# A residual layer scale on one core: the second of two early loads issued behind the entry barriers

## The chip, the cores and the metric

The kernel runs on one core of one Trainium2 chip. The metric is the device time of one execution in microseconds; the time before is 119.91 us, the median of 3 runs (119.89 to 119.97). The profile is of one more execution, whose span from the first to the last instruction of the program is 118.6 us, at a granted clock of 1.0.

## The reference

```python
B, S, D = 1024, 16, 512
x, y:  (B, S, D) bfloat16
gamma: (D,)      bfloat16

def reference(x, y, gamma):
    return x + gamma * y
```

Flattened, x, y and the output are 16,384 rows of 512 numbers, 16.78 MB each. Two are read and one is written: 50.33 MB in all. The arithmetic is one multiplication and one addition per element.

## The kernel before

Each of the 128 partitions gets 128 rows, in blocks of 8, 60 and 60. The transfers are two lists, one for SP's queue and one for the queue of ScalarE; an entry is a kind, and the rows from and to. VectorE has a list too: a multiplication ("m") in place in y_sb and an addition ("a") of x, piece by piece.

```python
BLOCKS = [8, 60, 60]
PIECES = [8, 15, 45, 60]

SP = [
    ('y', 0, 8),          # 1 MB, the first load
    ('y', 8, 68),         # 7.86 MB, the second load
    ('x', 8, 68, 0),
    ('y', 68, 128),
    ('x', 68, 128, 15),
    ('x', 0, 8, 0),
]
ACT = [('g',), ('s', 8, 68), ('s', 68, 128), ('s', 0, 8)]
EARLY = (2, 0)            # how many of SP's and of ScalarE's list go ahead of all else
HOLD = ('y', 0, 8)        # what lets the others go
RELEASE = ('x', 68, 128, 15)
DVE = [('m', 0), ('m', 1), ('m', 2), ('a', 2), ('a', 1), ('m', 3), ('a', 3), ('a', 0)]
```

The helper `ring` writes out one list. The entries from number n_early on are held behind a semaphore; the stores wait for `s_go` and for the additions.

```python
def ring(eng, what, n_early):
    known, went = 0, False
    for k, w in enumerate(what):
        kind = w[0]
        if k == n_early:
            _take(s_held[eng], 1, eng)       # wait for it, then take it back
        ...                                  # waits for buffers, additions, s_go
        elif kind == "y":
            r = slice(w[1], w[2])
            i = eng.dma_start(out=y_sb[:, r, :], in_=rows_of(yf, w[1], w[2])).then_inc(s_load[w], 16)
        ...
        if k < n_early:
            early.append(i.ins)

ring(nc.sync, SP, EARLY[0])
ring(nc.scalar, ACT, EARLY[1])
```

TensorE lets the held ones go when the first load has landed. It also spreads gamma over the partitions, by a product of a row of ones with gamma's row:

```python
nc.vector.memset(ones_row, 1.0).then_inc(s_ones, 1)
_take(s_load[HOLD], 16, nc.tensor)           # the first load has landed
for s_one in s_held.values():
    nc.tensor.sem_inc(s_one, 1)              # SP, ScalarE, VectorE may go on
_take(s_ones, 1, nc.tensor)
_take(s_gamma, 16, nc.tensor)
nc.tensor.matmul(gamma_ps, ones_row, gamma_row, start=True, stop=True).then_inc(s_ps, 1)
```

The program begins with entry barriers, at which all five engines wait for one another several times. They are not written in the kernel; they stand in the program's first block, with four small memsets on GpSimd. The last lines of the kernel take the early transfers out of its own block, which lies behind the barriers, and put them at the head of the first block, ahead of the barriers:

```python
main = nc.main_func.blocks[0].instructions
names = {i.name for i in early}
for b in nc.main_func.blocks[1:]:
    for i in [i for i in b.instructions if i.name in names]:
        b.instructions.remove(i)
for k, i in enumerate(early):
    main.insert(1 + k, i)
```

Of the kernel before, what the change touches and what calls it, by code (L numbers as in the profile page):

```python
# [11 lines left out]
SP = [  # L12
    ('y', 0, 8),
    ('y', 8, 68),
# [4 lines that stand above are left out]
]  # L19
ACT = [('g',), ('s', 8, 68), ('s', 68, 128), ('s', 0, 8)]  # L20

EARLY = (2, 0)

HOLD = ('y', 0, 8)

RELEASE = ('x', 68, 128, 15)

# [4 lines left out]
def _take(sem, n, eng):  # L32


    return eng.wait_ge(sem, n).then_inc(sem, -n)  # L35


def kernel(
# [9 lines left out]
    nc = tc.nc  # L48
# [16 lines left out]
    def rows_of(t, a, b):  # L65

        c = max(c for c in range(len(BLOCKS)) if edges[c] <= a)
        assert b <= edges[c + 1]
        block = t[P * edges[c] : P * edges[c + 1]].rearrange("(p n) d -> p n d", p=P)
        return block[:, a - edges[c] : b - edges[c], :]  # L70
# [25 lines left out]
    def pieces_of(a, b):  # L96
        return [c for c in range(n) if meets(starts[c], starts[c + 1], a, b)]
# [4 lines left out]
    def frees(w):  # L102

        c = set()
        for v in x_loads[: x_loads.index(w)]:
            lo, hi = max(v[3], w[3]), min(v[3] + v[2] - v[1], w[3] + w[2] - w[1])
            if lo < hi:
                c |= set(pieces_of(v[1] + lo - v[3], v[1] + hi - v[3]))
        return sorted(c)

    early = []

    def ring(eng, what, n_early):

        known, went = 0, False
        for k, w in enumerate(what):
            kind = w[0]
            if k == n_early:
                _take(s_held[eng], 1, eng)
            need = frees(w) if kind == "x" else pieces_of(w[1], w[2]) + list(w[3:]) if kind == "s" else []  # L120
            need = max((order[c] + 1 for c in need), default=0)
            if kind == "s" and not went:
                _take(s_go, 1, eng)
                went = True
            if need > known:
                eng.wait_ge(s_add, need)
                known = need
            if kind == "g":
                i = eng.dma_start(out=gamma_row, in_=gamma.unsqueeze(0)).then_inc(s_gamma, 16)
            elif kind == "x":  # L130
                to = x_sb[:, w[3] : w[3] + w[2] - w[1], :]
                i = eng.dma_start(out=to, in_=rows_of(xf, w[1], w[2])).then_inc(s_load[w], 16)
# [3 lines that stand above are left out]
            else:  # L136
                r = slice(w[1], w[2])
                i = eng.dma_start(out=rows_of(of, w[1], w[2]), in_=y_sb[:, r, :]).then_inc(s_out, 16)
            if k < n_early:
                early.append(i.ins)  # L140

    ring(nc.sync, SP, EARLY[0])
    ring(nc.scalar, ACT, EARLY[1])


    nc.vector.memset(ones_row, 1.0).then_inc(s_ones, 1)  # L146
    _take(s_load[HOLD], 16, nc.tensor)
    for s_one in s_held.values():
# [14 lines left out]
    def need(loads, c):  # L163
        for w in loads:
            if w not in landed and meets(starts[c], starts[c + 1], w[1], w[2]):
                if w == RELEASE:
                    _take(s_rel, 1, nc.vector)
                elif w == HOLD:
                    _take(s_held[nc.vector], 1, nc.vector)
# [64 lines left out]
```

## Time and profile before

| What | Value |
|---|---|
| Time, median of 3 | 119.91 us |
| Span of the profiled execution | 118.6 us |
| VectorE busy | 70.1 us (59%) |
| Moved by DMA | 50.33 MB, mean 424 GB/s over the span |
| First load: issued, landed | 0.00 us, 4.90 us |
| Second load: issued, landed | 0.42 us, 23.03 us |
| Last store: issued, landed | 96.52 us, 118.61 us |

In the profile's lines DVE is VectorE, PE is TensorE, POOL is GpSimd, SP and ACT are SyncE and ScalarE; a "q" behind a name is the engine's sequencer, which waits, passes barriers and issues transfers and is not counted as busy. L135 is a load of y, L132 of x, L129 of gamma, L138 a store, L35 a wait in the helper `_take`. L218 and L51 are the places of the entry barriers, their drains and their events. DMA packets are booked in the window in which they start. A line of the view by source begins with the line, engine and operation, then durations in ns (least, median, most), then the first and last start in us.

### The profile page before, as it was taken

To read this page: it belongs to the slowest core of one execution; us is meant where nothing else is said; L and a number is where in the kernel's file an instruction comes from. 1 tells how busy PE (TensorE), PEld (TensorE's weight loads), DVE (VectorE), ACT (ScalarE), POOL (GpSimd) and SP (SyncE) were. 2 spreads that over 40 slices of the span, in tenths; PEclk is the share of its full clock that TensorE was granted. 3 is DMA by queue.
4 is the path that set the end of the run, shared out by engine and by line. 5 is a ranking of instruction groups with operands and counts; after the bars stand their busy time and mean duration, and the time that the engine had idled before them with its cause. 6 is when DMAs were issued, how large, how long until landed. Compare 5 with 4: busy or idle time off the path is not lost. (4 is left out here: it accounts for less than half of the span.)

```text
span 118.6 us, 87 instructions
## 1 busy us (share of the span) xinstructions
PE 0.6 (0%) x1; PEld 0.1 (0%) x1; DVE 70.1 (59%) x10; POOL 0.2 (0%) x4
## 2 busy tenths in 40 slices
PE   0001000000000000000000000000000000000000
PEld 0000000000000000000000000000000000000000
DVE  0000720199999399999499999569999950000000
POOL 0000000000000000000000000000000000000000
DMA  5999799779779879879977977897997797797787
GB/s 182 503 560 435 331 394 601 331 331 663 331 331 642 352 331 621 373 331 394 601 331 331 663 331 331 384 633 331 414 580 331 331 663 331 331 663 331 331 367 318
DMA packets 1298, 50.33 MB, mean 424 GB/s; under 512 B 145, under 2 KB 146, under 8 KB 146
## 3 DMA queue, kind: packets, MB, share of 16 engines
q1 hardware_dynamic: 864, 33.55, 65.8%
q10 hardware_dynamic: 434, 16.78, 32.7%
HBM read 33.56 MB, written 16.78 MB: 424 GB/s over the span
## 5 line engine op out<-in xcount | busy, mean ns | idle before, releaser
L180 DVE TENSOR_TENSOR y_sb<-y_sb,gamma_sb 128x4096 bf16<-128x4096 bf16 (+3 forms) x4 | 34.7, 8690 | 9.7 <-DVEq L35 9.7
L189 DVE TENSOR_TENSOR y_sb<-x_sb,y_sb 128x23040 bf16<-128x23040 bf16 (+3 forms) x4 | 34.6, 8688 | 4.5 <-DVEq L35 4.5
L154 DVE CAST gamma_sb<-gamma_ps 128x512 bf16<-128x512 f32 x1 | 0.7, 692 | 10.1 <-DVEq L35 10.1
L146 DVE MEMSET ones_row<- 1x128 bf16 x1 | 0.2, 165 | 2.0 <-PEq L51 2.0
L152 PE MATMUL gamma_ps<-gamma_row,ones_row 1*128 1x512 bf16 x1 | 0.6, 578 | 11.6 <-PEq L35 11.6
L152 PEld LDWEIGHTS gamma_ps<-gamma_row,ones_row 1*128 1x128 bf16 x1 | 0.1, 100 | 11.5 <-issue 11.5
L218 POOL MEMSET const-uint8-127<- 128x1 uint8 x1 | 0.1, 102 | 0.0
L218 POOL MEMSET const-bfloat16-1.0<- 128x1 bf16 x1 | 0.1, 101 | 0.0
L218 POOL MEMSET const-float32-0.0<- 128x1 f32 x1 | 0.1, 98 | 0.2 <-issue 0.2
L218 POOL MEMSET const-float32-1.0<- 128x1 f32 x1 | 0.1, 98 | 0.0
## 6 DMA issues: line engine op xcount, KB each, us to landing
y_sb<-in_y_dram SPq DMA_DIRECT2D x2, 7680.0 KB, 38.2
x_sb<-in_x_dram SPq DMA_DIRECT2D x2, 7680.0 KB, 29.9
out_dram<-y_sb ACTq DMA_DIRECT2D x2, 7680.0 KB, 21.0
y_sb<-in_y_dram SPq DMA_DIRECT2D x1, 1024.0 KB, 4.9
x_sb<-in_x_dram SPq DMA_DIRECT2D x1, 1024.0 KB, 22.3
out_dram<-y_sb ACTq DMA_DIRECT2D x1, 1024.0 KB, 22.1
gamma_row<-in_gamma_dram ACTq DMA_DIRECT2D x1, 1.0 KB
```

The source lines that it names most:

```text
L146: nc.vector.memset(ones_row, 1.0).then_inc(s_ones, 1)
L152: nc.tensor.matmul(gamma_ps, ones_row, gamma_row, start=True, stop=True).then_inc(s_ps, 1)
L154: nc.vector.tensor_copy(out=gamma_sb, in_=gamma_ps).then_inc(s_dve, 1)
L180: nc.vector.tensor_tensor(out=yt, in0=yt, in1=g, op=MULT).then_inc(s_dve, 1)
L189: nc.vector.tensor_tensor(out=yt, in0=xt, in1=yt, op=ADD).then_inc(s_add, 1)
L218: nc = _bacc.Bacc("TRN2", target_bir_lowering=False, num_devices=1)
```

## The change

Only one load instead of two is put ahead of the barriers. The hold stays where it was, ahead of the third entry: it gets a number of its own, AHEAD. The second load is thus issued in the kernel's own block, behind the barriers, without waiting for any semaphore of the kernel. Its place in SP's order stays the same. It is meant to let SP come to the barriers sooner, with only the first load's issue ahead of them.

```diff
-EARLY = (2, 0)
-
-HOLD = ('y', 0, 8)
+EARLY = (1, 0)
+
+HOLD, AHEAD = ('y', 0, 8), (2, 0)
 ...
-    def ring(eng, what, n_early):
+    def ring(eng, what, n_early, n_ahead):
 ...
-            if k == n_early:
+            if k == n_ahead:
                 _take(s_held[eng], 1, eng)
 ...
-    ring(nc.sync, SP, EARLY[0])
-    ring(nc.scalar, ACT, EARLY[1])
+    ring(nc.sync, SP, EARLY[0], AHEAD[0])
+    ring(nc.scalar, ACT, EARLY[1], AHEAD[1])
```

SP's instructions then stand in this order: first load, barriers and branch, second load, wait for the hold, x load, and so on. The other engines' instructions are the same as before.

## The prediction, made before the changed kernel was run

> **What bounds the kernel now.** I read the page from the top: busy times first, then the slices, then the queues. They say at once that no engine bounds this kernel. The busiest is VectorE:
>
> ```profile
> PE 0.6 (0%) x1; PEld 0.1 (0%) x1; DVE 70.1 (59%) x10; POOL 0.2 (0%) x4
> ...
> DMA  5999799779779879879977977897997797797787
> ...
> q1 hardware_dynamic: 864, 33.55, 65.8%
> q10 hardware_dynamic: 434, 16.78, 32.7%
> ```
>
> Queue q1 carries the loads (two tensors of 16.78 MB), q10 gamma and the stores. Together they fill 65.8 + 32.7 = 98.5% of the 16 DMA engines' time over the span. The sevens in the row of slices are no idle time: a packet of 61,440 bytes takes 2.27 us and is booked where it starts, so a slice of 3 us catches one or two rounds of them. Over a longer stretch this averages out. The view by windows (columns: stretch, length, busy time of PE, PEld, DVE and POOL, clock, DMA share, GB/s) gives:
>
> ```profile
> 0.00:1.00 1.00, 0.00 (x0) 0.00 (x0) 0.00 (x0) 0.20 (x4) 1.00 0.00 0
> ...
> 1.00:2.00 1.00, 0.00 (x0) 0.00 (x0) 0.01 (x1) 0.00 (x0) 1.00 0.74 131
> ...
> 2.00:118.60 116.60, 0.58 (x1) 0.10 (x1) 70.11 (x10) 0.00 (x0) 1.00 1.00 431
> ```
>
> The reader is to see three things. In the first microsecond no byte moves. In the second, packets are open but only 131 GB/s flow. From 2.0 us on, the DMA share is 1.00 up to the end, at 431 GB/s. So the kernel is 50.33 MB of traffic behind a start-up of about 2 us, and only what delays the start of that stream, or tears a hole in it, can change the time.
>
> The page's chain of the work that ended last covers only 16% of the span (issue 12%, DVE 4%), because it doesn't follow the transfers; I leave it aside. What VectorE waits for shows in the groups, and it has slack: its last addition ends at 96.48 us, and the last 38.6 us (from the landing of the last load at 79.96 us) are stores alone: 16.78 MB / 38.6 us = 435 GB/s, the full rate.
>
> The start is in the timeline (start, duration, engine, operation):
>
> ```profile
> 0.00 0.85 SPq L135 DMA_DIRECT2D y_sb<-in_y_dram  x2
> ...
> 1.99 0.17 DVE L146 MEMSET ones_row<- 1x128 bf16 x1 [1.99 <-PEq L51]
> 5.23 0.33 SPq L132 DMA_DIRECT2D x_sb<-in_x_dram  x1
> 5.43 0.52 ACTq L129 DMA_DIRECT2D gamma_row<-in_gamma_dram  x1
> ```
>
> Both early loads are issued before the barriers (0.00 to 0.37 and 0.42 to 0.85 us). VectorE passes the barriers at 1.9 us and does its memset. Nothing else is issued until the first load, 1 MB, has landed at 4.90 us.
>
> And the entry barrier waits for SP, which comes late because it issues two transfers first:
>
> ```profile
> L218 PEldq DRAIN  x1: 8/8/8, 0.3 to 0.3; - x1
> ...
> L218 SPq DRAIN  x1: 125/125/125, 0.9 to 0.9; - x1
> ```
>
> The other engines are at their drain by 0.3 us (GpSimd's ends at 0.48), SP's runs from 0.90 to 1.03 us. The barriers that follow take from there to 1.84 us on SP.
>
> **What the Trainium skill says.** "DMA: Bandwidth & Descriptors", section "Queues, rings and completion order", says that each issuing engine owns one ring on each of the 16 DMA engines and that descriptors are consumed in ring order. The trace agrees: on all 16 engines the first load's eight packets of 8,192 bytes come first, then those of the second load. The second load therefore can't start earlier than the first is through, however early it was issued. "Perfetto Trace Analysis", section "DMA Instruction — HWDGE (DVE, Sync)", says that the recorded span of an issuing instruction is the making of descriptors, and that data moves after or beside it; here the issue lasts 0.37 us and the first packet starts at 1.02 us. "DMA: Bandwidth & Descriptors", section "Latency and other measured facts", puts the first byte of such a transfer at about 0.6 us; 1.02 - 0.37 = 0.65 us agrees.
>
> **The change, part by part.**
>
> 1. *It removes* one issue of 0.42 us, plus a gap of 0.05 us, from SP's way to the first barrier. SP's drain then starts near 0.43 instead of 0.90 us. GpSimd's drain at 0.48 becomes the last to arrive, or close to it, so the barriers end some 0.45 us earlier: 1.84 - 0.45 = 1.4 us on SP. This is worth nothing by itself. Behind the barriers lie only a memset and waits that the first load ends at 4.9 us.
>
> 2. *It moves* the second issue to behind the last barrier. VectorE shows what a step out of it costs: 0.13 us from its last barrier event to its memset. So the issue runs from about 1.5 to 1.9 us, against 0.42 to 0.85 before, 1.1 us later.
>
> 3. *When do its descriptors stand in the rings?* Take the pattern of the first load, the only one issued to idle DMA engines: eight engines start a packet 1.02 to 1.09 us after the issue began, the other eight 1.71 to 1.82 us after. For the second load that gives 1.5 + 1.0 = 2.5 us to 1.5 + 1.8 = 3.3 us.
>
> 4. *When are they needed?* In the trace's packets, each engine ends its eight packets of the first load between 4.17 and 4.55 us and takes a packet of 61,440 bytes at once. Margin: 4.17 - 3.3 = 0.9 us on the worst pairing of engines, 4.17 - 2.5 = 1.7 us on the better one. Neither is used up, so no hole opens.
>
> 5. *Everything after* hangs on the first load's landing (4.90 us) and on the order in SP's ring, which stays the same: second load, then x, then the third load of y. Nothing moves.
>
> Sum: 0 from the barriers, 0 from the later issue. 119.91 us stays 119.9, with one open term that the next part names.
>
> **The rivals.**
>
> *A: a hole between the first and the second load.* If the second issue comes later than 1.5 us, or its descriptors take longer than the first load's, engines stand idle from 4.2 us until they arrive. Every microsecond of that goes whole into the end. For it: the first load is short, 1 MB, some 2.4 us at full rate. Against it: it takes 0.9 us more delay than I reckon before the first engine runs dry. A miss by 1.2 us would make 120.2 us.
>
> *B: the start of the first load becomes faster.* Half of the engines start their first packet only at 1.71 us or later, and the eight early ones hold theirs for 0.97 to 1.30 us where every later one takes 0.31. In just this time, from 0.42 us, SP has the second transfer's descriptors made. If these two are in each other's way, the change frees the first load, it lands earlier than 4.90 us, and the whole stream moves up with it: 0.1 to 0.6 us, so 119.3 to 119.8 us. For it: the coincidence in time. Against it: all 16 engines are through their first packet between 2.03 and 2.31 us whether they began early or late, which looks like one common latency of a first read, not a queue for descriptors. I think this likelier than A, which puts the middle slightly under the time before.
>
> *C: the earlier barriers bring something.* Then the memset at 1.99 us would have to matter. It doesn't: TensorE needs it only with gamma, which lands at 11.43 us, and VectorE's first multiplication at 13.24 us is 105 us ahead of the end, with transfers saturated throughout. This rival makes no difference to the time.
>
> **Range and chances.** The centre is 119.91 minus 0.06 for B at small odds: 119.85 us. Downward the range holds most of B (half a microsecond: 119.4); upward a small hole or a slightly different rate (0.3 us: 120.2). To leave the 2% band it would take 2.4 us, more than the whole start-up lasts, or a hole as long as the whole first load; 1% on either side is ample.
>
> **What would show it.** In the changed profile: SP's drain near 0.4 us and VectorE's memset near 1.5 us (step 1); one issue at 0.00 and one at about 1.5 us (step 2); window 2.0 us to the end at a DMA share of 1.00 and 431 GB/s (steps 3 and 4); the first load landing at 4.9 us and the x issue at 5.2 us (step 5). A share under 1.00 between 4 and 10 us would prove A; a landing of the first load at 4.3 to 4.8 us, with all engines started by 1.5 us, would prove B. The prediction is wrong if the second issue lands far behind 1.5 us, or if the two issues do disturb each other by more than half a microsecond.

## The result, and the profile after

The changed kernel takes **121.62 us** (median of 6 runs, 121.12 to 121.69) against 119.96 us before in the same runs (119.89 to 120.11). The ratio is 1.0128, with a 95% interval of 1.011 to 1.0147: slower by 1.7 us, outside the predicted range of 119.4 to 120.2 us.

The page of the changed kernel, in the lines that answer to those shown of before:

```profile
PE 0.6 (0%) x1; PEld 0.1 (0%) x1; DVE 70.1 (58%) x10; POOL 0.2 (0%) x4
...
q1 hardware_dynamic: 864, 33.55, 65.2%
q10 hardware_dynamic: 434, 16.78, 32.4%
```

The work is the same to a tenth of a microsecond. The queues fill 97.6% of the span in place of 98.5%: 1.8 us longer, with the same bytes. Its timeline and its view by source of the barrier's lines show that what I predicted of the issues came true:

```profile
0.00 1.76 SPq L135 DMA_DIRECT2D y_sb<-in_y_dram  x2
...
1.52 0.17 DVE L146 MEMSET ones_row<- 1x128 bf16 x1 [1.52 <-PEq L51]
5.24 0.33 SPq L132 DMA_DIRECT2D x_sb<-in_x_dram  x1
```

```profile
L218 SPq DRAIN  x1: 131/131/131, 0.4 to 0.4; - x1
```

SP drains at 0.42 us, VectorE's memset comes at 1.52 us (1.99 before), the second load is issued from 1.43 to 1.76 us, and x at 5.24 us, as before. (The timeline joins both loads into one row of 1.76 us.) What I predicted of the stream did not: from 2.0 us to the end the DMA share is 0.98 at 423 GB/s, and not 1.00 at 431.

```profile
2.00:120.40 118.40, 0.58 (x1) 0.10 (x1) 69.96 (x9) 0.00 (x0) 1.00 0.98 423
```

The sign that I had named for rival A, a share under 1.00 between 4 and 10 us, would have missed it. Before, then after:

```profile
4.00:10.00 6.00, 0.00 (x0) 0.00 (x0) 0.00 (x0) 0.00 (x0) 1.00 1.16 501
```

```profile
4.00:10.00 6.00, 0.00 (x0) 0.00 (x0) 0.00 (x0) 0.00 (x0) 1.00 1.06 431
```

Since a packet is booked whole where it starts, so short a window can read over 1.00 although engines stand idle in it. Only the comparison with before shows that something is missing. Windows chosen to fit the rounds of packets find the time in two places. From 4.60 to 6.20 us nothing may start, because each engine should be inside its first packet of 61,440 bytes; before, then after:

```profile
4.60:6.20 1.60, 0.00 (x0) 0.00 (x0) 0.00 (x0) 0.00 (x0) 1.00 0.00 0
```

```profile
4.60:6.20 1.60, 0.00 (x0) 0.00 (x0) 0.00 (x0) 0.00 (x0) 1.00 0.14 38
```

38 GB/s over 1.6 us is 61 KB: one engine takes up its first packet of the second load only now (at 5.11 us in the packet records). The second place lies 75 us later; again before, then after:

```profile
79.40:80.40 1.00, 0.00 (x0) 0.00 (x0) 1.00 (x1) 0.00 (x0) 1.00 1.00 430
```

```profile
79.40:80.40 1.00, 0.00 (x0) 0.00 (x0) 0.53 (x1) 0.00 (x0) 1.00 0.28 115
```

There most DMA engines stand idle for a microsecond, between the loads and the stores. (0.28 counts the packets that start there; with each packet spread over its duration, the engines are busy for 0.39 of that microsecond.)

I added up the packets of both traces, each spread over its duration, and compared when the same amount had been moved:

| Moved | Before | After | Behind |
|---|---|---|---|
| 1 MB | 4.18 us | 4.08 us | -0.09 us |
| 2 MB | 6.50 us | 6.89 us | 0.39 us |
| 4 MB | 11.11 us | 11.63 us | 0.52 us |
| 32 MB | 75.71 us | 76.18 us | 0.47 us |
| 34 MB | 80.37 us | 81.59 us | 1.22 us |
| 50 MB | 117.25 us | 118.60 us | 1.35 us |
| last store landed | 118.61 us | 120.32 us | 1.71 us |

Half a microsecond is lost where the engines pass from the first to the second load (below: the handover), nothing for 28 MB, 0.75 us where they pass from loads to stores (the seam), 0.13 us in the stores, and 0.36 us at the end, where the last engine lags.

The lag begins at the handover. The 16 engines report the second load's landing one by one: before, 22.65 to 23.03 us, all within 0.38 us; after, 22.73 to 23.50 us for 15 of them, and 24.77 us for the last, 1.27 us behind the fifteenth. This distance stays: 1.27, 1.28 and 1.29 us at the next three loads. Nobody takes over the late engine's work in these loads. The last of these loads is the one that lets the stores go. It landed at 79.23 us on the last engine and at 77.94 us on the fifteenth. The stores were therefore issued at 79.58 us, and their first packet came 0.87 us later, when most engines had run dry.

### The profile page after: what moved, and what is told of

The parts are those of the page before. It is cut to its first block, busy times and chain, and to the rows that moved or that the text cites. A ratio compares the mean times of both kernels' runs of the same rounds, so it can differ in the third digit from the quotient of the medians.

```text
span 120.4 us, 87 instructions
## 1 busy us (share of the span) xinstructions
PE 0.6 (0%) x1; PEld 0.1 (0%) x1; DVE 70.1 (58%) x10; POOL 0.2 (0%) x4
```

## The experiments

In the tables "extra" is by how much the first packet of 61,440 bytes lasted longer than the usual 2.27 us, in the mean of the 16 engines, from the packet records (2.23 us for packets of 60,416 bytes, 2.12 us for 57,344). It is the profiled execution's; times are medians of several. It leaves out time in which an engine stood idle ahead of that packet, so it is a sign of the loss at the handover and not its size: in a second profile of the changed kernel it is only 0.16 us, although the stream was 0.58 us behind at 4 MB. In the diffs, `...` marks lines left out, and the line that allocates `s_pad` is shown once.

### Place or moment?

`both_behind` issues both loads behind the barriers; `apart_ahead` issues both ahead of them, with a pause between.

```diff
 both_behind, against the changed kernel
-EARLY = (1, 0)
+EARLY = (0, 0)
 apart_ahead, against the changed kernel
-EARLY = (1, 0)
+EARLY = (2, 0)
+PADS = 24
 ...
+    s_pad = sem("s_pad")          # a semaphore that nothing waits for
 ...
+            if k == 1 and eng is nc.sync:
+                early.extend(eng.sem_inc(s_pad, 1).ins for _ in range(PADS))
```

> Both early loads are issued behind the entry barriers, 0.4 us apart as in the kernel before; nothing is left ahead of the barriers. Theory 'gap' (the second load's descriptors need some 2.6 to 3.5 us from the issue until data flows, on one engine nearly 5 us, and the first load is through before that when its issue is 1.4 us earlier): here the two issues are close together again, so no engine falls behind; the 16 landings of the second load lie within 0.4 us of one another and the time is that of the kernel before plus the later start, 120.0 + 1.4 = 121.4 us. Theory 'place' (a transfer issued behind the barriers is served worse): an engine falls behind as in the changed kernel and the time is over 122.3 us. Theory 'stream' (making descriptors while the engines move data disturbs them): as 'gap', for no data moves at the second issue.

> Both early loads stand ahead of the barriers as in the kernel before, but 24 increments of an unused semaphore on SP stand between their issues, so that the second one comes about 1 us later (some 1.4 to 2 us after the first). Theories 'gap' and 'stream': an engine falls behind by about a microsecond at the second load, its landings spread over 1 to 2 us, and the time is 121 to 122 us. Theory 'place': 119.9 to 120.1 us, as in the kernel before, with landings within 0.4 us.

`both_behind` took 121.27 us, ratio 1.011 (1.0093 to 1.0127): just the later start. Its timeline:

```profile
1.38 0.85 SPq L135 DMA_DIRECT2D y_sb<-in_y_dram  x2
1.47 0.17 DVE L146 MEMSET ones_row<- 1x128 bf16 x1 [1.47 <-PEq L51]
6.50 0.33 SPq L132 DMA_DIRECT2D x_sb<-in_x_dram  x1
```

Both issues stand together again, 1.38 us later than before, and 119.93 + 1.38 = 121.31. The extra is 0.00 us and the second load's landings lie within 0.55 us (I had expected 0.4), as wide as the first load's own. `apart_ahead` issued the second load at 1.83 us and took 120.84 us (11 runs, 120.08 to 121.54), ratio 1.0075 (1.0049 to 1.01), extra 0.45 us. Its median lies just under what I expected, and its spread is wide. So the barriers are not needed for the loss: it comes with the time between the two issues alone. To be sure, the same moment as in the changed kernel, but ahead of the barriers (17 increments):

> The same with 17 increments: the second load is issued at about 1.43 us, the moment at which the changed kernel issues it, but ahead of the barriers and not behind them. If the moment is all that counts: as the changed kernel, 120.9 to 121.7 us with landings of the second load spread by 0.7 us or more. If standing behind the barriers adds something of its own: under 120.5 us.

121.24 us, ratio 1.0111 (1.007 to 1.0152), issued at 1.43 us, extra 0.51 us. It is a loss like the changed kernel's without the change of place; its four runs lie from 120.63 to 121.90 us. Its window:

```profile
4.60:6.20 1.60, 0.00 (x0) 0.00 (x0) 0.00 (x0) 0.00 (x0) 1.00 0.62 230
```

230 GB/s over 1.6 us is 368 KB: six engines begin late here, and not one.

And with the same distance, both behind the barriers:

```diff
 against apart17
-EARLY = (2, 0)
+EARLY = (0, 0)
 ...
-                early.extend(eng.sem_inc(s_pad, 1).ins for _ in range(PADS))
+                for _ in range(PADS):
+                    eng.sem_inc(s_pad, 1)
```

> Both loads behind the barriers with 17 increments between them, so the second one is issued about 1.4 us after the first, which itself starts at 1.4 us. With both close together behind the barriers the time was 121.27 us. If the limit is the distance from the first issue: the loss comes on top, 0.7 to 1.9 us, 122.0 to 123.1 us. If the limit were tied to the start of the program and not to the first issue: 121.2 to 121.5 us.

122.53 us, ratio 1.0229 (1.0197 to 1.0262), extra 0.68 us: the loss, 1.26 us against `both_behind`, comes on top of the later start. The limit moves with the first issue, or with the first packets, which start 1.0 us after it in both kernels, and not with the start of the program.

### Where is the limit?

The same kernel with 8, 12 and 45 increments in place of 24.

> As the run with both loads ahead of the barriers and 24 increments between them, but with 8 increments: the second load is issued at about 0.9 us, some 3.3 us before the first engine is through with the first load (4.17 us before). Theory 'gap' with a need of 2.6 to 3.5 us on most engines: nearly no loss, 119.9 to 120.4 us. If any distance of more than the 0.4 us of before hurts: 120.6 us or more.

> Both loads ahead of the barriers, 12 increments between them: the second load is issued at about 1.14 us. With 8 increments (0.91 us) nothing was lost, with 24 (1.83 us) 0.9 us. If the limit is the first packets' start at 1.0 us: a loss already, 120.4 to 121.2 us. If the limit is a distance of some 3 us to the end of the first load at 4.17 us: just no loss, 119.9 to 120.2 us.

> As before, with 45 increments: the second load is issued at about 3.05 us, 1.1 us before the first engine is through. Theory 'gap' as a plain latency of some 3.3 us: the stream stands still until about 6.4 us and loses some 2.1 us, so 121.9 to 122.5 us. If the loss at the second load is a fixed cost of a start while other packets flow, and not a latency from the issue: 120.5 to 121.5 us, as with 24 increments.

| Second issue at | Time | Ratio (95%) | Extra |
|---|---|---|---|
| 0.91 us | 119.94 us | 1.0001 (0.9993 to 1.001) | 0.03 us |
| 1.13 us | 120.00 us (20 runs) | 1.0035 (1.0015 to 1.0055) | 0.00 us |
| 1.43 us | 121.24 us | 1.0111 (1.007 to 1.0152) | 0.51 us |
| 1.83 us | 120.84 us | 1.0075 (1.0049 to 1.01) | 0.45 us |
| 3.06 us | 120.77 us | 1.0073 (1.0057 to 1.0089) | 0.50 us |

At 0.91 us the second load's delay costs nothing. At 1.13 us the runs fall into two groups: 12 of 20 at 119.87 to 120.08 us, 8 at 120.70 to 121.31 us (the profiled one is of the first group). From 1.43 us on every run is slower than the slowest of before in the same series, but for one at 1.83 us that equals it. The first load's first packets start at 0.99 to 1.02 us in these traces, so the edge lies close to the moment at which the engines begin to work. Whether that moment makes it, or the distance between the issues, these runs don't separate. Both expectations for 1.13 us were half right, in different runs. For 3.06 us my main expectation was wrong: 1.2 us later than 1.83 us, and no dearer. It isn't a plain latency from the issue, which would have grown with every microsecond.

When the second load's data began to flow shows it better. I estimate that moment for each engine by taking the usual 2.27 us back from the end of its first long packet. Before, it is 4.2 to 4.6 us. With the second issue at 1.43, 1.83 and 3.06 us it is 4.6 to 5.6, 4.2 to 5.4 and 4.5 to 5.2 us: nearly the same moment, within about a microsecond of the first load's last packets (they end at 3.9 to 4.5 us), whatever the issue. In the last of these that is only 1.5 to 2.1 us after the issue.

### Is it a matter of distance to the end of the first load?

The first load gets 16 rows (2 MB) in place of 8; and once 10 rows.

```diff
 big_before and big_after: EARLY = (2, 0) and (1, 0)
-BLOCKS = [8, 60, 60]
-PIECES = [8, 15, 45, 60]
+BLOCKS = [16, 56, 56]
+PIECES = [16, 16, 40, 56]
 big_apart57 and big_apart80: the same with EARLY = (2, 0), PADS = 57 and 80
 first10: EARLY = (1, 0)
+BLOCKS = [10, 59, 59]
+PIECES = [10, 15, 44, 59]
 (the two lists' rows follow)
```

> The first load is 16 rows (2 MB) in place of 8, the other blocks 56 rows each; both early loads ahead of the barriers. It is the other half of the next run. All theories: landings of the second load within 0.5 us; the time near that of the kernel before, 119.7 to 120.5 us.

> As the run before it (first load of 2 MB), with the second load issued behind the barriers. The engines are busy with the first load until about 6.6 us, so the second load's descriptors have 5 us from their issue at 1.4 us. Theory 'gap': they are there in time; within 0.2 us of the run before it, and no engine behind. Theory 'stream' (descriptors are made while the engines move data, whatever the margin): 0.7 to 1.7 us slower than the run before it, with an engine behind. Theory 'place': the same as 'stream'.

> The changed kernel with a first load of 10 rows in place of 8 (the other blocks 59 rows each). The second load is issued at 1.42 us as in the changed kernel, but the engines are busy with the first load until about 4.8 us, so the distance from the issue to the end of the first load is 3.4 us and not 2.8 us. Theory 'distance' (no loss where the second load is issued 3.3 us or more before the first load ends, a loss of 0.5 to 0.9 us below some 2.8 us): no loss at the start, 119.9 to 120.3 us. Rival 'before the first packet' (the second load has to be issued before the first packets flow at 1.0 us, unless the first load is very long): 120.6 us or more, with the window from 4 to 9 us at less than a DMA share of 1.00 or landings of the second load spread by over 0.7 us.

> The 2 MB first load again, both loads ahead of the barriers, with 57 increments between them: the second load is issued at about 3.75 us, some 2.9 us before the engines are through with the first load at 6.6 us. Theory 'distance': the loss comes back, 0.4 to 0.9 us over the same kernel without the increments (120.63 us): 121.0 to 121.6 us. If a long first load hides the second one's start whatever the distance: 120.5 to 120.9 us.

> The 2 MB first load with 80 increments: the second load is issued at about 5.1 us, 1.5 us before the first engines are through with the first load. With 57 increments (2.9 us) the change from the first to the second load cost nothing. A latency of 2 to 3 us from the issue: the loss is there, 0.5 us or more between the second and the fourth megabyte, 121.5 us or more. If long packets at the end of the first load hide the start at any distance: the change still costs nothing, 120.7 to 121.4 us.

| Kernel | Second issue at | First engine takes up the second load at | Time | Ratio (95%) | Extra |
|---|---|---|---|---|---|
| big_before | 0.42 us | 6.40 us | 120.63 us | 1.006 (1.0045 to 1.0075) | 0.00 us |
| big_after | 1.42 us | 6.63 us | 120.81 us | 1.0077 (1.0062 to 1.0092) | 0.00 us |
| big_apart57 | 3.77 us | 6.63 us | 121.18 us | 1.0105 (1.0086 to 1.0124) | 0.00 us |
| big_apart80 | 5.60 us | 6.60 us | 121.89 us | 1.0183 (1.0134 to 1.0233) | 0.29 us |
| first10 | 1.43 us | 4.70 us | 120.39 us | 1.0042 (1.0025 to 1.0058) | 0.16 us |

With the 2 MB load the change as such costs next to nothing: 120.81 against 120.63 us, intervals that overlap, no extra. (This layout is itself 0.7 us slower than the 1 MB one; why stays open.) Here the second issue falls while packets flow, so making descriptors beside moving data doesn't cost anything by itself: the theory 'stream' of the expectations falls. But a rule of distance, counted from the second issue to the moment at which the first engine is free for it, fails too. 2.9 us were enough here (57 increments), while with 10 rows 3.3 us left an extra of 0.16 us, and 2.3 us in the changed kernel (3.70 less 1.43 us) left 0.53. (How much of the 0.4 us by which `first10` is slower is its layout's is not shown: there is no run of it with both loads early.) With 80 increments the second load was issued later than I had reckoned, 1.0 us ahead of that moment, and the extra is back; its data began to flow 1.5 to 2.1 us after the issue, as with the issue at 3.06 us above. In its profile about 0.3 us are lost at the handover and 1.2 us at the seam, where `big_before` loses 0.5. So a longer first load hides the start of the second; how much time it needs isn't one number. `big_apart57` lost 0.55 us against `big_before` all the same: in its profile one engine starts the first load itself only at 2.24 us and lands 0.7 us behind the others. That lag doesn't come from the handover and stays unexplained.

### Other causes that were tried

Three other transfers are issued at 5.2 to 6.1 us, just when the second load begins. `quiet` puts them off:

```diff
+    for _ in range(20):
+        nc.tensor.sem_inc(s_pad, 1)
     for s_one in s_held.values():
         nc.tensor.sem_inc(s_one, 1)
```

> The changed kernel, but TensorE counts up an unused semaphore 20 times before it lets the held transfers go, so that the x load, gamma and the third load of y are issued near 8 us and not at 5.2 to 6.1 us, when the second load has just begun. They aren't needed before 23 us. Theory 'gap' (the second load's own descriptors are late): the start is as slow as in the changed kernel, an engine behind by about 1 us, 121.1 to 121.8 us. Rival 'crowd' (the three issues at 5.2 us disturb the second load's first packets): no engine behind and a time of 119.8 to 120.3 us.

121.10 us, ratio 1.01 (1.0085 to 1.0115), extra 0.62 us, with the x load at 8.19 us. The crowd is not the cause.

`first_halves` splits the first load into two of 4 rows, which makes its packets half as long:

> The changed kernel with the first load split into two of 4 rows, both ahead of the barriers: 16 packets of 4,096 bytes on an engine in place of 8 of 8,192, so the last packets are half as long. The big load is issued behind the barriers, at about 1.9 us. Theory 'last packets' (the engine begins to make ready for the next load a few packets before the end[...]): the change costs more than in the changed kernel, 0.8 to 1.2 us at the start, 121.6 to 122.3 us. If packets' length doesn't count: as with both loads 1.83 us apart, 120.5 to 121.5 us.

120.67 us, ratio 1.006 (1.0044 to 1.0077), extra 0.24 us: half of the changed kernel's and not twice as much. By the idea that the last packets' length sets the cost it should have grown; it didn't. (The long load is issued at 1.90 us here.)

`other_ring` has ScalarE issue the second load:

```diff
-    ('y', 8, 68),          # on SP's list
+    ('g',),
-ACT = [('g',), ...
+ACT = [('y', 8, 68), ...
-HOLD, AHEAD = ('y', 0, 8), (2, 0)
+HOLD, AHEAD = ('y', 0, 8), (1, 1)
```

> As the changed kernel, but the second load is issued by ScalarE, first thing behind the barriers (at about 1.4 us), so that it stands on ScalarE's ring and not behind the first load on SP's; gamma takes its place on SP's list, held as before. The engines take packets of both rings in turn, so the first load lands late (about 15 us) and the x load is issued then, still well before the second load is through. Theory 'ring' (the cost is that of adding to a ring that is being worked on): no loss at the change, 119.8 to 120.3 us, DMA share 1.00 from 2 to 9 us. Theory 'engine' (any later second transfer costs it): 120.5 to 121.7 us.

132.25 us, ratio 1.1033 (1.1001 to 1.1065), which neither theory foresaw. Its timeline shows where that comes from:

```profile
1.43 0.37 ACTq L135 DMA_DIRECT2D y_sb<-in_y_dram  x1
...
5.68 0.35 SPq L132 DMA_DIRECT2D x_sb<-in_x_dram  x1
6.07 0.51 SPq L135 DMA_DIRECT2D y_sb<-in_y_dram  x1
...
40.88 16.23 DVE L180 TENSOR_TENSOR y_sb<-y_sb,gamma_sb 128x7680 bf16<-128x7680 bf16 x2 [25.18 <-DVEq L35]
...
69.44 4.40 SPq L132 DMA_DIRECT2D x_sb<-in_x_dram  x2
```

I had expected the two rings to take turns during the first load. They didn't: it landed at 4.99 us as ever, SP went on at once with x and the third load of y, and those took turns with the second load, which landed at 40.75 us in place of 24.77. VectorE began its large multiplications 16 us later than in the changed kernel (40.88 against 24.90 us), SP waited until 69.44 us for the additions that free x's buffer, and from 60 to 72 us the engines moved 0.5 MB in all. For the handover only the start counts: the extra is 0.69 us, and the stream, 0.13 us ahead of the kernel before at 1 MB, is 0.75 us behind it at 3 MB. So the loss doesn't need a common ring.

### The seam

```diff
 late_stores, against the kernel before
+    for _ in range(8):
+        nc.tensor.sem_inc(s_pad, 1)
     nc.tensor.sem_inc(s_go, 1)
```

> The kernel before, but TensorE counts up an unused semaphore 8 times, about 1.2 us, before it lets the stores go. It puts the wait of the changed kernel's seam into the kernel before without touching the start. In the kernel before the stores are issued at 77.83 us and the loads run dry near 79.4 us; a store's first packet comes about 1.0 to 1.3 us after its issue. If the seam counts: the engines idle for some 0.7 to 1.1 us near 80 us and the time is 120.6 to 121.1 us. If other slack takes it up: 119.9 to 120.1 us.

120.61 us, ratio 1.0055 (1.004 to 1.007), at the low edge of what I expected. The stores are issued at 78.93 us and not at 77.83, and the windows show a hole followed by all engines' first packets of the stores, which start from 79.79 us on (spread over their durations, packets fill only 0.13 of the stretch from 79.4 to 79.9 us):

```profile
79.00:79.50 0.50, 0.00 (x0) 0.00 (x0) 0.28 (x1) 0.00 (x0) 1.00 0.25 98
79.50:80.00 0.50, 0.00 (x0) 0.00 (x0) 0.50 (x1) 0.00 (x0) 1.00 4.61 1966
```

A load that lets the stores go 1.1 us late thus costs 0.6 to 0.7 us with an undisturbed start. The other way round, the stores released earlier in the changed kernel:

```diff
-    ('x', 68, 128, 15),
+    ('x', 68, 120, 15),
+    ('x', 120, 128, 67),
-RELEASE = ('x', 68, 128, 15)
+RELEASE = ('x', 68, 120, 15)
```

> The changed kernel, but the load of x rows 68 to 128 is split into 52 and 8 rows and the first of them lets the stores go, about 2.3 us earlier. That takes away the part of the loss that lies at the seam of loads and stores: in the changed kernel most engines stood idle from 79.4 to 80.4 us because the load that lets the stores go had one engine 1.27 us behind. If that is right: about 0.7 us faster than the changed kernel, 120.7 to 121.1 us, with no idle engines near 79 us, and the loss at the start as before. If the seam is no loss of its own: 121.4 to 121.8 us.

121.28 us, ratio 1.0115 (1.0096 to 1.0134). Less than the changed kernel's 121.62, more than expected, and the same as the 121.27 of the changed kernel's second series below. The engines are busy at 79 us, but in the profiled execution no engine had fallen far behind (the landings of the second load lie within 0.69 us), so it doesn't tell how much of the changed kernel's seam it would mend. Inconclusive.

### The changed kernel once more

> The changed kernel once more, for a second profile of it. Theory 'straggler' (one engine that is over a microsecond behind at the second load is a constant part of the loss): again 121.1 to 121.7 us, and a landing of the second load in which the last engine is over 1 us behind the one before it. If the straggler is a matter of chance: the same range of times, with landings spread by 0.6 to 0.9 us in this profile, and engines idle for less than 0.4 us at the seam of loads and stores.

121.27 us (120.97 to 121.72), ratio 1.0113 (1.0086 to 1.014). The one straggler of the first profile is not a constant part of the loss. Here four engines began the second load about a microsecond late, and the landings spread over 1.17 us (0.31 at the first load). The stream was 0.58 us behind at 4 MB, much as in the first profile, but the seam added only 0.17 us. In these two profiles the loss at the handover is of much the same size (0.52 and 0.58 us behind at 4 MB); how it is shared out over the engines differs, and with it what it costs later. In the other runs with an issue at 1.4 us and a first load of 8 rows on one ring it lies between 0.64 us (`early_stores`) and 0.93 us (`quiet`).

## Why the prediction was wrong, step by step

- **Step 1 (earlier barriers, worth nothing): right.** SP's drain at 0.42 us, the memset at 1.52 us; the `apart8` run came through its barriers later than before (memset at 2.38 us) and took 119.94 us, so their moment doesn't count either way. Rival C falls with it.
- **Step 2 (issue from 1.5 to 1.9 us): right** within 0.15 us: 1.43 to 1.76 us.
- **Step 3 (descriptors in the rings 1.0 to 1.8 us after the issue) and step 4 (a margin of 0.9 us, no hole): wrong, and this is the failed step.** I took the first load's start, on idle engines, for that of a second load on busy ones. By the estimate above, the second load of the changed kernel began to flow at 4.06 to 4.92 us on 15 engines and at 6.33 us on one, 2.6 to 4.9 us after the issue; in its second profile at 4.19 to 5.71 us. Rival A was thus what happened, but its arithmetic, too, was that of a plain latency, and the run with the issue at 3.06 us shows that it isn't one: there 1.5 to 2.1 us were enough from the issue to the data, nearly what step 3 had, and the hole was as large. The term that I put at 0 was 0.5 to 0.6 us.
- **Step 5 ("Nothing moves"): wrong.** The landing of the first load and the x issue did stay (4.91 and 5.24 us). But I had read the landing of a transfer as one event. It is the slowest of 16, and the lag of the last one stayed to the end of the loads. That put another 0.75 us at the seam and 0.36 us at the end of the profiled execution. `late_stores` shows the seam's part by itself.
- **Rival B (the first load frees itself): not shown.** In the changed kernel's first profile the first packets of the eight early engines took 0.31 to 0.38 us in place of 0.97 to 1.30, and the first quarter of a megabyte was moved 0.28 us earlier; but the lead was 0.09 us at 1 MB and gone at 1.25 MB. In the second profile these packets took 0.55 to 1.24 us, and there was no lead.

What stays open is why a load issued after the engines have begun costs this at the handover. Shown are: it needs no barrier, no crowd and no common ring; for issues from 1.4 to 3.1 us it hardly depends on when; a first load of 2 MB hides it, unless the issue comes as late as 1.0 us before the handover. What goes on inside the DMA engines these runs don't tell.

No version tried beats the kernel before. The nearest, with the second issue at 0.91 us, equals it.

## What to carry to other kernels

In a kernel like this one, put a second transfer into the rings before the engines start on the first one, or make the first one long (which here cost 0.7 us by its layout): with a first load of 1 MB a distance of 0.4 to 0.9 us between the issues was free, and 1.4 us cost 1.1 to 1.7 us of time. Where the stream is saturated, read the landing of a transfer engine by engine: one that falls behind can keep its lag for the rest of the loads, as here, and every wait on the full count waits for it. And don't take a latency from an idle machine for a busy one; look for a transfer in the trace that was issued under the same load. And test the sign by which you mean to know a rival: a share over a short window of packets booked at their start can hide the very hole that it is to show.

## What the runs showed of the hardware that I had not expected

- A lag of the last DMA engine of 1.27 us at 24.8 us was still 1.29 us at 79.2 us. Behind the seam, where the others had waited, it was 0.5 to 0.6 us.
- With a second load on another ring, issued at 1.43 us, its first packet of 61,440 bytes started at 3.73 us, 2.3 us after the issue, though the first load's packets flowed from 1.0 to 4.64 us. The Trainium skill, "DMA: Bandwidth & Descriptors", section "Queues, rings and completion order", says that an engine takes turns between the rings that have work; here that turn came only when the first load was nearly through. Whether the second load's descriptors stood ready any earlier, the trace doesn't tell, so this does not contradict the page. Between long transfers the rings did take turns: from 8 to 36 us 96 long packets of SP's queue and 99 of ScalarE's started.
- Where most engines had just run dry, the first packet of the stores came 0.86 to 0.87 us after their issue (three traces: the changed kernel's two and `late_stores`), against 1.0 us for the very first load.
